# Last block of an S4 + gated FFN kernel: two halves of a slot group transposed apart with zero-padded tables, and a quarter of the residual sum moved to TensorE and ScalarE

## The chip, the cores and the metric

The kernel runs on one core of a Trainium2 chip. The metric is the device time of one execution in microseconds (us); lower is better. Engines are named as in the profile: PE is TensorE (PEld its weight loads), DVE is VectorE, ACT is ScalarE, POOL is GpSimd, SP is SyncE, which here only issues DMAs.

## The reference

`x` is normalised over its 512 channels. Each channel is convolved with its own long kernel `K`, made from 128 complex modes, by FFTs of twice the length; beside it a two-layer GELU network runs on the same normalised input. The output is the input plus the product of the two:

```python
xn = _layernorm(x, axis=-1)
s = _A_ref(xn, ...)    # K[d,l] = Re sum_n C*dt*B * exp(dt*A*l);  y = irfft(rfft(xn) * rfft(K))[:L] + xn * Dskip
g = _silu(_B_ref(xn, w1, b1, w2, b2))    # gelu(xn @ w1 + b1) @ w2 + b2
return x + s * g
```

With L = 2048 rows, D = 512 channels, 128 modes, 1792 hidden units; all in fp32.

## The kernel before, in words

The first part (until about 390 us) runs the network, normalisation and the tables of `K`, in an order written out by hand (`ORDER`). Its result `g` is put in DRAM (`gd`).

The second part does the convolution. Channels are taken in four blocks of 128 (NB = 4), and the FFT is factored as 32 x 64 (N1 x N2). In a block the work goes through eight slots: `second_dft` (L911) makes the spectra of input and kernel on PE, `spectrum` copies one of the two from PSUM to SBUF (ACT, `uh`, L919), `product` and `combine` multiply the spectra on DVE (L929, L937, L939) into `Y`, one `Y` for two slots (`Y_0` to `Y_3`). The way back follows: `back_dft` (L948) transforms `Y_j` on PE into two PSUM banks `sa`; `back_out` (L959) copies them into the SBUF tile `Z` (kh = 0 for j = 0, 1; kh = 1 for j = 2, 3); `turn` (L968) is a DVE transpose of 32 x 32 blocks from `Z` into `T`, in two halves s = 0, 1 (rows q 0 to 7 and 8 to 15 of the output); `last_dft` (L988) multiplies `T` with the table `gc` into the result `y` in PSUM: 16 products, one for each of the 16 parts of 32 x 32 of the PE array (g picks the rows, w the columns), first those of kh = 0, then those of kh = 1 on top. At last `y` is multiplied with `g` (DVE), `x` is added, and the sum is stored.

The order on each engine is that of the code, since the region is recorded with a manual schedule. For blocks 0 to 2 the way back lies beside the next block's slots. For the last block it has nothing beside it, and is written out at the end of the kernel (L1197 to L1243):

- `back_dft` of `Y_3` is cut into two halves (`h0`, `h1`), which write parts of the same two banks, so the second half waits until ACT has copied the first one out.
- The four rows of `y` are cut into two halves of q. The first half has its PSUM tiles `wide` (two for all four channel groups), the second half four banks (`py[1]`).
- `last_dft` of kh = 0 for the first half, four products of the identity with itself that write into a bank that is overwritten next (L1211), `last_dft` of kh = 0 for the second half, and kh = 1 for both.
- On DVE: the copy of one bank of `Y_3`'s second half (L959), the two transposes of kh = 1 (L968), then the products with `g` (`gated`, L1226 and L1223) and half of the additions of `x` (`added`, L1230). The other half of the additions is on POOL (L1230). In `parts(s, n)`, s is the half of q and n the half of the 128 channels; `added(s, 0)` is POOL's, `added(s, 1)` DVE's.
- Stores t = 0, 1 hold the first half of q, t = 2, 3 the second half; t = 0 and 2 are issued by SP, 1 and 3 by ACT.

Of the kernel before, what the change touches and what calls it, by code (L numbers as in the profile page):

```python
# [11 lines left out]
F32 = mybir.dt.float32  # L12
# [8 lines left out]
P = 128  # L21
L, D, NS, F = 2048, 512, 128, 1792
G = D // P
NF = F // P
KD = D // P
N1, N2 = 32, 64
NB = 4
# [5 lines left out]
NQ = L // P  # L33
# [95 lines left out]
def _shape_constants():  # L129
    n1 = np.arange(N1)[:, None]  # L130
    k1 = np.arange(N1)[None, :]
    a = 2 * np.pi * n1 * (k1 + 0.25) / N1
    cf = np.zeros((G, N1, 2, 2, N1))
    for g in range(G):
        cf[g, :, g % 2] = np.stack([np.cos(a), -np.sin(a)], 1)
    cg = np.stack([np.cos(a).T, -np.sin(a).T], 1).reshape(2, 2, 4, 2, 2, N1)
    cg = np.tile(cg.transpose(1, 3, 2, 4, 0, 5).reshape(1, N1, 2, N1), (G, 1, 1, 1))
    n2 = np.arange(N2)[:, None]
    k2 = np.arange(N2)[None, :]
    cm = np.zeros((2, N2, N1, 2, N2))  # L140
    ct = np.zeros((2, N2, N1, 2, N2))
    for k in range(N1):
        th = 2 * np.pi * (n2 * (k + 0.25) / L + n2 * k2 / N2)
        c, s = np.cos(th), np.sin(th)
        cm[:, :, k, 0, :] = c
        cm[:, :, k, 1, :] = s
        ct[0, :, k, 0, :] = c.T / L
        ct[1, :, k, 0, :] = -s.T / L
        ct[0, :, k, 1, :] = s.T / L
        ct[1, :, k, 1, :] = c.T / L  # L150
# [7 lines left out]
    return {  # L158
        "cf": cf.reshape(P, 4 * N1).astype(f),
        "cg": cg.reshape(P, 2 * N1).astype(f),  # L160
        "cm": cm.reshape(P, N1 * 2 * N2).astype(f),
        "ct": ct.reshape(P, N1 * P).astype(f),
        "cb": cb.reshape(CH * NPC, CH * NPH).astype(ml_dtypes.bfloat16),
    }
# [3 lines left out]
def kernel(  # L168
# [5 lines left out]
    V, A, GP, PE, SY = nc.vector, nc.scalar, nc.gpsimd, nc.tensor, nc.sync  # L174
# [613 lines left out]
    def open_mid():  # L788
        SB["pm"] = pm = opened(p2, "pm", "right")
        SB["ps"] = opened(pz, "psm", "left", bufs=2, space=PSUM)  # L790
        SB["tcn"] = pm.tile([P, N1, P], F32, name="tcn")
        SB["tb"] = SB["tcn"].rearrange("p (k o) m -> p k o m", o=2)
        xf[1] = pm.tile([P, 2, 2, N1, N2], F32, tag="X1", name="X1")
        SB["uh"] = pm.tile([P, 2, 2, P], F32, tag="uh", name="uh_0_0", bufs=2)
        SB["t0"] = pm.tile([P, 2, 2, 4, N2], F32, tag="t0", name="t0_0_0", bufs=2)
        SB["gc"] = pm.tile([P, 2, N1], F32, name="gc")
        gx[0] = new_tail(0)
        yy[0, "T", 1] = new_turn(0, 1)

# [141 lines left out]
    def back_dft(b, j, es=slice(0, 4)):  # L941
        if (b, j, "p") not in yy:
            yy[b, j, "p"] = [bank(f"sa{b}_{j}_{a}") for a in range(2)]
        for e in range(4)[es]:
            for o in range(2):
                for a, p in enumerate(yy[b, j, "p"]):
                    r = slice(64 * a, 64 * a + 64)
                    PE.matmul(p[:, e, :], yy[b, j][r, o, e, :], SB["tb"][r, 4 * j + e, o, :],  # L948
                              start=(o == 0), stop=(o == 1), skip_group_check=True)

    def back_out(b, j, es=slice(0, 4), engs=(A, A)):
        kh = j // 2
        if (b, "Z", kh) not in yy:
            yy[b, "Z", kh] = SB["pm"].tile([P, N2, N1 // 2, 2], F32, tag=f"Z{kh}", name=f"Z{b}_{kh}")
        for a, (p, eng) in enumerate(zip(yy[b, j, "p"], engs)):
            k = 8 * (j % 2) + 4 * a
            src = p.rearrange("p k (x c) -> p x k c", c=2)[:, :, es]
            dst = yy[b, "Z", kh][:, :, k:k + 4, :][:, :, es]
            eng.copy(dst, src) if eng is A else eng.tensor_copy(dst, src)  # L959

    def new_turn(b, kh):
        return SB["pm"].tile([P, 4, 2, 8, N1], F32, tag=f"T{kh}", name=f"T{b}_{kh}")

    def turn(b, kh, s):
        if (b, "T", kh) not in yy:
            yy[b, "T", kh] = new_turn(b, kh)
        Z = yy[b, "Z", kh].rearrange("p (w s q) k c -> p w s q (k c)", w=4, s=2)
        V.transpose(yy[b, "T", kh][:, :, s], Z[:, :, s])  # L968

    gx = {}  # L970

# [10 lines left out]
    def last_dft(b, kh, py, q=slice(0, NQ)):  # L982
        T = yy[b, "T", kh].rearrange("p w s q i -> p w (s q) i")
        for w in range(4):
            for g in range(G):
                r, m = slice(g * N1, (g + 1) * N1), slice(w * N1, (w + 1) * N1)
                o = py[g].rearrange("p (q i) -> p q i", i=N1)
                PE.matmul(o[m], SB["gc"][r, kh], T[r, w, q], start=(kh == 0), stop=(kh == 1), skip_group_check=True)  # L988
# [173 lines left out]
    with tc.manual_schedule():  # L1162
        SB["spare"] = False
        open_front()
        z_load(NTB - 1)
        for j in range(4):
            mc_load(j)
        side_skip(0)
        side_turn(1, eng=GP)
        SB["spare"] = True  # L1170
        for p in "S0 F00 S1 S2 F01 S3 L0 F10 L1 A0 F11 A1 L2 L3 A2 A3".split():
            if p[0] == "F":
                k = int(p[1]), int(p[2])
# [12 lines left out]
        z_store(NTB - 1)  # L1186
        SB["spare"] = False
        fa.close()
        open_mid()
        ct_load(0)  # L1190
        SY.dma_start(SB["gc"].rearrange("p h n -> p (h n)"), cg)
        for b in range(NB - 1):
            for i in range(4):
                two_slots(b, i)
        for g in range(8):
            slot(NB - 1, g)
        b = NB - 1  # L1197
        h0, h1 = slice(0, 2), slice(2, 4)
        back_dft(b, 3, h0)
        back_out(b, 3, h0)  # L1200
        wide = [SB["ps"].tile([P, 2, 4 * P], F32, tag="ri", name=f"y{b}_{n}", bufs=2) for n in range(2)]
        py = [[wide[g // 2][:, g % 2, :2 * P] for g in range(G)]]
        halves = [slice(0, NQ // 2), slice(NQ // 2, NQ)]
        back_dft(b, 3, h1)
        back_out(b, 3, h1, (A, V))
        last_dft(b, 0, py[0], halves[0])
        py.append([bank(f"y{b}_{g}_1").rearrange("p e m -> p (e m)")[:, :2 * P] for g in range(G)])
        for s in range(2):
            turn(b, 1, s)
        for n in range(4):  # L1210
            PE.matmul(py[1][0][:, :P], ident, ident, start=True, stop=True, skip_group_check=True)  # L1211
        last_dft(b, 0, py[1], halves[1])
        for s in range(2):
            last_dft(b, 1, py[s], halves[s])
        gt, xt_ = gx[b]
        def parts(s, n):
            return tuple(t[:, halves[s], 64 * n:64 * n + 64] for t in (gt, xt_))

        def gated(s, n):
            if s:  # L1220
                for g in (2 * n, 2 * n + 1):
                    gg = gt[:, halves[1], g * N1:g * N1 + N1]
                    V.tensor_mul(gg, py[1][g].rearrange("p (q i) -> p q i", i=N1), gg)  # L1223
            else:
                gp = parts(0, n)[0].rearrange("p q (g i) -> p g q i", i=N1)
                V.tensor_mul(gp, wide[n][:, :, :2 * P].rearrange("p g (q i) -> p g q i", i=N1), gp)  # L1226

        def added(s, n):
            gv, xv = parts(s, n)
            (V if n else GP).tensor_add(xv, gv, xv)  # L1230

        gated(0, 0)
        added(0, 0)
        gated(0, 1)
        gated(1, 0)
        added(0, 1)
        for t in range(2):
            store(b, t, (SY, A)[t % 2])
        gated(1, 1)
        for n in range(2):  # L1240
            added(1, n)
        for t in range(2, 4):
            store(b, t, (SY, A)[t % 2])  # L1243
    pz.close()
# [32 lines left out]
```

## Time and profile before

| what | value |
|---|---|
| time, median of 3 runs (lowest, highest) | 533.06 us (532.49, 534.91) |
| the profiled execution's own time | 532.96 us |
| its span, first to last instruction | 531.1 us |
| mean granted PE clock | 0.995 |
| share of the span busy: PE, PEld, DVE, ACT, POOL | 97%, 80%, 81%, 74%, 49% |
| last PE product of the kernel starts | 523.0 us |
| second pair of stores issued | 527.1 us |

Times within the profile are counted from the start of the span. A row of the timeline gives the start, the length, the engine with its line, the operation, `out<-in` by the program's names, the shapes, and `x` with the number of instructions merged in it; in brackets stands the idle time of the engine ahead of it and what ended that. Instructions on one engine are pipelined, so two that are merged take less than the sum of their single lengths. Each fp32 product of PE appears as two records (and two weight loads).

### The profile page before, as it was taken

The numbers are of one execution on the slowest core, as the hardware profiler recorded it, in microseconds if no ns is written. First come the engines' busy times: TensorE is split into PE (matmuls) and PEld (weight loads), VectorE is DVE, ScalarE is ACT, GpSimd is POOL, SyncE is SP. The second block draws the span as 40 slices with busy tenths as digits, with TensorE's granted clock in tenths as the row PEclk, the third lists the DMA queues.
The fourth block names the chain that finished last, engine by engine and source line by source line (L and its number), as shares of the span: only waits on it lengthen the run. The fifth ranks groups of instructions, "written<-read, shape, count | busy, mean of one in ns | idle before, by whom it ended". The sixth has DMA issues, their size and how long they took to land.

```text
span 531.1 us, 16527 instructions
## 1 busy us (share of the span) xinstructions
PE 516.4 (97%) x6999; PEld 422.4 (80%) x6999; DVE 429.7 (81%) x726; ACT 390.8 (74%) x556; POOL 260.7 (49%) x384
## 2 busy tenths in 40 slices
PE   8899999999999999999999999999999999999993
PEld 8677787877777777877777787778889998998882
DVE  6989899999998789787875886898257779677896
ACT  3588996999987988888778799799454573663330
POOL 5619478667597569669817175645301002103042
PEclk9999999999999999999999999999999999999998
DMA  7946527762427966418135532591656639542552
GB/s 221 307 121 195 187 94 233 241 199 77 161 80 198 352 215 180 140 29 252 41 108 175 185 59 107 133 176 45 233 209 224 77 102 214 164 166 81 195 193 97
DMA packets 86086, 85.84 MB, mean 162 GB/s; under 512 B 41878, under 2 KB 60698, under 8 KB 84988
## 3 DMA queue, kind: packets, MB, share of 16 engines
q1 hardware_dynamic: 76944, 66.43, 42.3%
q0 software_dynamic: 8768, 17.83, 10.8%
q8 instruction: 55, 0.90, 0.7%
q10 hardware_dynamic: 300, 0.53, 0.3%
q14 instruction: 19, 0.16, 0.1%
HBM read 51.22 MB, written 33.55 MB: 160 GB/s over the span
## 4 chain that ended last, share of the span: by engine, by line
PE 84%; DVE 6%; ACT 3%; POOL 3%; DMA 2%; issue 2%; POOLq 0%; DVEq 0%; ACTq 0%
PE s L911 11%; PE z L287 9%; PE z L289 8%; PE z L288 8%; PE f L248 8%; PE f L250 8%; PE f L249 8%; PE s L889 6%; PE sa L948 6%; PE kg L655 5%; PE ph L591 3%; PE y L988 2%; DMA w1s<-in_B_w_dram 1%; DVE hl L274 1%; PE xT L359 1%
## 5 line engine op out<-in xcount | busy, mean ns | idle before, releaser
L616 POOL TENSOR_TENSOR mm<-mm,rc 128x32 f32<-128x32 f32 (+4 forms) x150 | 97.1, 647 | 11.8
L287 PE MATMUL z<-w2h,hh 128*128 128x512 f32 x224 | 95.6, 427 | 0.0
L248 PE MATMUL f<-xh,w1h 128*128 128x512 f32 x220 | 91.7, 417 | 0.9 <-ACT w1h L231 0.6
L250 PE MATMUL f<-xh,w1l 128*128 128x512 f32 x220 | 87.1, 396 | 2.2 <-DVE w1l L233 1.5
L289 PE MATMUL z<-w2h,hl 128*128 128x512 f32 x224 | 87.7, 392 | 0.1
L288 PE MATMUL z<-w2l,hh 128*128 128x512 f32 x224 | 87.7, 391 | 0.0
L249 PE MATMUL f<-xl,w1h 128*128 128x512 f32 x220 | 86.8, 394 | 0.0
L605 DVE SCALAR_TENSOR_TENSOR ra<-ra,ph 128x512 f32<-128x512 f32 x64 | 43.8, 684 | 19.4 <-ACT ra L599 18.5
L911 PE MATMUL s<-X,mc 64*64 64x128 f32 x1536 | 58.0, 272 | 0.4 <-DVE t L929 0.4
L929 DVE TENSOR_TENSOR t<-s,uh 128x512 f32<-128x512 f32 x64 | 40.9, 684 | 15.1 <-ACT uh L919 11.6
L250 PEld LDWEIGHTS f<-xh,w1l 128*128 128x128 f32 x220 | 41.3, 188 | 12.4 <-DVE w1l L233 2.4
L639 DVE TENSOR_TENSOR e<-mm,ra 128x1024 f32<-128x1024 f32 x32 | 42.7, 1336 | 10.0 <-ACT ra L627 4.2
L248 PEld LDWEIGHTS f<-xh,w1h 128*128 128x128 f32 x220 | 41.5, 189 | 11.4 <-ACT w1h L231 1.1
L262 ACT ACTIVATE f<-f,b1s 128x512 f32<-128x512 f32 x56 | 37.2, 665 | 18.1 <-PE f L250 16.9
L289 PEld LDWEIGHTS z<-w2h,hl 128*128 128x128 f32 x224 | 42.1, 188 | 10.1 <-DVE hl L274 0.5
L613 POOL COPY mm<-rc 128x32 f32<-128x32 f32 x30 | 15.5, 516 | 69.5 <-DVE e L646 39.6
L287 PEld LDWEIGHTS z<-w2h,hh 128*128 128x128 f32 x224 | 42.4, 189 | 8.9 <-issue 0.3
L911 PEld LDWEIGHTS s<-X,mc 64*64 64x64 f32 x1536 | 44.8, 133 | 5.3 <-issue 1.5
L288 PEld LDWEIGHTS z<-w2l,hh 128*128 128x128 f32 x224 | 42.2, 189 | 8.2
L249 PEld LDWEIGHTS f<-xl,w1h 128*128 128x128 f32 x220 | 41.3, 188 | 9.1
L919 ACT COPY uh<-s 128x512 f32<-128x512 f32 x32 | 18.8, 587 | 40.1 <-PE s L911 22.0
L274 DVE TENSOR_TENSOR hl<-f,hh 128x512 fp32r<-128x512 f32 x56 | 37.8, 682 | 10.6 <-ACT hh L268 10.6
(183 smaller groups left out, 1130.9 us busy)
## 6 DMA issues: line engine op xcount, KB each, us to landing
x<-in_A_u_dram SPq DMA_DIRECT2D x8, 512.0 KB
xs<-x SPq DMA_DIRECT2D x8, 512.0 KB
xt_h<-xh POOLq DMA_DIRECT2D x4, 1024.0 KB, 5.7
xt_l<-xl POOLq DMA_DIRECT2D x4, 1024.0 KB, 8.2
kgd<-ko SPq DMA_DIRECT2D x16, 256.0 KB
za<-zo SPq DMA_DIRECT2D x4, 1024.0 KB
xh<-xt_h POOLq DMA_DIRECT2D x4, 1024.0 KB, 6.7
xl<-xt_l POOLq DMA_DIRECT2D x4, 1024.0 KB, 10.0
```

Source lines behind the costliest of these rows:

```text
L248: PE.matmul(p, wh[:, k, :], xh[:, k, :], start=(k == 0), stop=False)
L249: PE.matmul(p, wh[:, k, :], xl[:, k, :], start=False, stop=False)
L250: PE.matmul(p, wl[:, k, :], xh[:, k, :], start=False, stop=(k == KD - 1))
L274: V.tensor_sub(hl, hf, hh)
L287: PE.matmul(z, hh[:, s], wh, start=(f0 == 0 and not rows), stop=False)
L288: PE.matmul(z, hh[:, s], wl, start=False, stop=False)
L289: PE.matmul(z, hl[:, s], wh, start=False, stop=(f0 == FA - 1))
L605: V.scalar_tensor_tensor(ra[:, 0, c], ra[:, 1, c], MAGIC, p, op0=ALU.subtract, op1=ALU.subtract)
L616: GP.tensor_mul(mv[:, :, 0:3:2, w:2 * w], mv[:, :, 0:3:2, 0:w], rc[:, 2 + 2 * i:4 + 2 * i, :].rearrange("p j c -> p c j").unsqueeze(3).to_ ...
L639: V.tensor_mul(e1, m1.unsqueeze(1).to_broadcast([P, 2, CH, N1]), ra[:, :, :, :N1])
L911: PE.matmul(p[ka * 64:(ka + 1) * 64, r, o, :, jj], w, xf[b][h, c, :, k, :], start=(c == 0), stop=(c == 1), skip_group_check=True)
L929: V.tensor_mul(t, p[:, i, :, 1].unsqueeze(1).to_broadcast([P, 2, 2, P]), uh)
```

## The change

The change touches only the end of the last block and one table.

- `cg`, the table behind `gc`, gets four more slices of 32 x 32 (2 to 5) beside the two that it had: for j = 0, 1 and o = 0, 1 a copy of half of kh = 1's table in one half of the rows and zeros in the other. The load of `gc` grows from 32 KB to 96 KB.
- In the last block `back_out` puts slots 4, 5 (j = 2) and slots 6, 7 (j = 3) of kh = 1 into two separate halves of `Z`. `turn_pairs` transposes one half of `Z` for one half of q: four DVE transposes of 128 x 512 stand for two of 128 x 1024. The ones of slots 4, 5 no longer need `Y_3`.
- `last_pairs` multiplies each transposed piece with the two padded tables, e = 0, 1, one after the other into alternate groups of 32 columns of `y`: for a half of q and one j, 32 products of 128 columns. Slots 4, 5 and 6, 7 are added up in PSUM, so there are 4 x 32 such products where there were 2 x 16 of 256 columns.
- On PE the first half's `last_dft` of kh = 0 goes between the two halves of `back_dft` of `Y_3`, and the four identity products are gone.
- ACT, not DVE, copies the second bank of the second half of `Y_3`.
- The addition of `x` for the second half of q, n = 0, is no longer POOL's: PE multiplies the identity with that quarter of `x`, then with the gated product, into one PSUM tile (128 x 512), and ACT copies the sum to SBUF. The addition for the first half of q, n = 1, goes from DVE to POOL. DVE keeps one addition, the last.

PE, at the end of the last block. `sa_3_0` and `sa_3_1` are the two banks of `back_dft` of `Y_3`; `y_0`, `y_1` are the tiles of the first half of q, `y_0_1` to `y_3_1` those of the second half; `T_0` and `T_1` are the transposed tiles of kh = 0 and 1. Before:

```order
L948 MATMUL sa_3_0_7183<-tcn,Y_3_7115 128x128
L948 MATMUL sa_3_1_7184<-tcn,Y_3_7115 128x128
L988 MATMUL y_0_7195<-T_0_7074,gc 32x256 x2
L988 MATMUL y_1_7196<-T_0_7074,gc 32x256 x2
...
L1211 MATMUL y_0_1_7223<-ident 128x128 x4
L988 MATMUL y_0_1_7223<-T_0_7074,gc 32x256
...
L988 MATMUL y_0_7195<-T_1_7227,gc 32x256 x2
...
L988 MATMUL y_3_1_7226<-T_1_7227,gc 32x256
```

Of the change, from the first half of `Y_3`'s products on:

```order
L954 MATMUL sa_3_1_7184<-tcn,Y_3_7115 128x128
L1014 MATMUL y_0_7195<-T_0_7074,gc 32x256 x2
...
L954 MATMUL sa_3_0_7183<-tcn,Y_3_7115 128x128
...
L994 MATMUL y_0_7195<-T_1_7221,gc 32x4x32 x4
...
L1014 MATMUL y_0_1_7258<-T_0_7074,gc 32x256
...
L994 MATMUL y_0_1_7258<-T_1_7221,gc 32x4x32 x2
...
L1264 MATMUL o_7379<-last,ident 128x512
L1267 MATMUL o_7379<-last,ident 128x512
```

Sixteen products moved ahead of the second half of `Y_3`, the identity products on `y_0_1` went, each row of `T_1` now stands for twice as many products of half the width, and two products of the identity with `last` (the tile that holds `g` and `x`) follow at the end.

DVE, from the second transpose of kh = 0 to its last instruction (`Z_1` is the tile `Z` of kh = 1). Before:

```order
L968 STREAM_TRANSPOSE T_0_7074<-Z_0_7061 128x4x256
L959 COPY Z_1_7175<-sa_3_1_7184 128x64x4
L968 STREAM_TRANSPOSE T_1_7227<-Z_1_7175 128x4x256 x2
L1226 TENSOR_TENSOR last<-y_0_7195,last 128x2x8x32
L1226 TENSOR_TENSOR last<-y_1_7196,last 128x2x8x32
L1223 TENSOR_TENSOR last<-y_0_1_7223,last 128x8x32
L1223 TENSOR_TENSOR last<-y_1_1_7224,last 128x8x32
L1230 TENSOR_TENSOR last<-last 128x8x64
L1223 TENSOR_TENSOR last<-y_2_1_7225,last 128x8x32
L1223 TENSOR_TENSOR last<-y_3_1_7226,last 128x8x32
L1230 TENSOR_TENSOR last<-last 128x8x64
```

Of the change:

```order
L978 STREAM_TRANSPOSE T_0_7074<-Z_0_7061 128x4x256
L985 STREAM_TRANSPOSE T_1_7221<-Z_1_7175 128x512 x4
L1254 TENSOR_TENSOR last<-y_0_7195,last 128x2x8x32
L1254 TENSOR_TENSOR last<-y_1_7196,last 128x2x8x32
L1251 TENSOR_TENSOR last<-y_0_1_7258,last 128x8x32
L1251 TENSOR_TENSOR last<-y_1_1_7259,last 128x8x32
L1251 TENSOR_TENSOR last<-y_2_1_7260,last 128x8x32
L1251 TENSOR_TENSOR last<-y_3_1_7261,last 128x8x32
L1258 TENSOR_TENSOR last<-last 128x8x64
```

The copy is gone, the two transposes became four of half the size, and one of the two additions left.

The diff, without the table's shape lines:

```diff
+    pair = np.zeros((G, 2, 2, 2, N1 // 2, N1))
+    for j in range(2):
+        for o in range(2):
+            pair[:, j, o, o] = cg[:, N1 // 2 * j:N1 // 2 * (j + 1), 1]
...
@@ back_out @@
+            if b == NB - 1 and kh:
+                Z = yy[b, "Z", kh].rearrange("p x k c -> p (x k c)").rearrange("p (j x k c) -> p j x k c", j=2, k=N1 // 4, c=2)
+                dst = Z[:, j % 2, :, 4 * a:4 * a + 4, :][:, :, es]
...
+    def turn_pairs(b, j, s):
+        Z = yy[b, "Z", 1].rearrange("p x k c -> p (x k c)").rearrange("p (j w s q) -> p j w s q", j=2, w=4, s=2)
+        T = yy[b, "T", 1].rearrange("p w s q i -> p (w s q i)").rearrange("p (j s w q) -> p j s w q", j=2, s=2, w=4)
+        V.transpose(T[:, j, s], Z[:, j, :, s])
+
+    def last_pairs(b, j, py, s):
+        T = yy[b, "T", 1].rearrange("p w s q i -> p (w s q i)").rearrange("p (j s w q) -> p j s w q", j=2, s=2, w=4)
+        for w in range(4):
+            for g in range(G):
+                r, m = slice(g * N1, (g + 1) * N1), slice(w * N1, (w + 1) * N1)
+                o = py[g].rearrange("p (q e i) -> p q e i", e=2, i=N1)
+                for e in range(2):
+                    PE.matmul(o[m, :, e], SB["gc"][r, 2 + 2 * j + e], T[r, j, s, w], start=False, stop=(j == 1), skip_group_check=True)
...
         back_dft(b, 3, h0)
         back_out(b, 3, h0)
...
+        last_dft(b, 0, py[0], halves[0])
         back_dft(b, 3, h1)
-        back_out(b, 3, h1, (A, V))
-        last_dft(b, 0, py[0], halves[0])
+        for s in range(2):
+            turn_pairs(b, 0, s)
+        back_out(b, 3, h1)
+        last_pairs(b, 0, py[0], 0)
...
-        for s in range(2):
-            turn(b, 1, s)
-        for n in range(4):
-            PE.matmul(py[1][0][:, :P], ident, ident, start=True, stop=True, skip_group_check=True)
         last_dft(b, 0, py[1], halves[1])
         for s in range(2):
-            last_dft(b, 1, py[s], halves[s])
+            turn_pairs(b, 1, s)
+        last_pairs(b, 1, py[0], 0)
+        for j in range(2):
+            last_pairs(b, j, py[1], 1)
...
         gated(0, 1)
+        full = SB["ps"].tile([P, 2, 4 * P], F32, tag="ri", name=f"o{b}", bufs=2)[:, 0].rearrange("p (q i) -> p q i", i=64)
+        PE.matmul(full, ident, parts(1, 0)[1], start=True, stop=False)
         gated(1, 0)
-        added(0, 1)
+        gv, xv = parts(1, 0)
+        PE.matmul(full, ident, gv, start=False, stop=True)
+        A.copy(xv, full)
+        GP.tensor_add(parts(0, 1)[1], parts(0, 1)[0], parts(0, 1)[1])
         for t in range(2):
             store(b, t, (SY, A)[t % 2])
         gated(1, 1)
-        for n in range(2):
-            added(1, n)
+        added(1, 1)
```

More of the change, by code (lines that the diff above doesn't have):

```diff
@@ L137, in _shape_constants @@
     cg = np.tile(cg.transpose(1, 3, 2, 4, 0, 5).reshape(1, N1, 2, N1), (G, 1, 1, 1))
+    pair = np.zeros((G, 2, 2, 2, N1 // 2, N1))
+    for j in range(2):
+        for o in range(2):
+            pair[:, j, o, o] = cg[:, N1 // 2 * j:N1 // 2 * (j + 1), 1]
+    pair = pair.reshape(G, 4, N1, N1).transpose(0, 2, 1, 3)
+    cg = np.concatenate([cg, pair], 2)
     n2 = np.arange(N2)[:, None]
@@ L159, in _shape_constants @@
         "cf": cf.reshape(P, 4 * N1).astype(f),
-        "cg": cg.reshape(P, 2 * N1).astype(f),
+        "cg": cg.reshape(P, 6 * N1).astype(f),
         "cm": cm.reshape(P, N1 * 2 * N2).astype(f),
@@ L795, in open_mid @@
         SB["t0"] = pm.tile([P, 2, 2, 4, N2], F32, tag="t0", name="t0_0_0", bufs=2)
-        SB["gc"] = pm.tile([P, 2, N1], F32, name="gc")
+        SB["gc"] = pm.tile([P, 6, N1], F32, name="gc")
         gx[0] = new_tail(0)
@@ L957, in back_out @@
             src = p.rearrange("p k (x c) -> p x k c", c=2)[:, :, es]
-            dst = yy[b, "Z", kh][:, :, k:k + 4, :][:, :, es]
+            if b == NB - 1 and kh:
+                Z = yy[b, "Z", kh].rearrange("p x k c -> p (x k c)").rearrange("p (j x k c) -> p j x k c", j=2, k=N1 // 4, c=2)
+                dst = Z[:, j % 2, :, 4 * a:4 * a + 4, :][:, :, es]
+            else:
+                dst = yy[b, "Z", kh][:, :, k:k + 4, :][:, :, es]
             eng.copy(dst, src) if eng is A else eng.tensor_copy(dst, src)
@@ L968, in turn @@
         V.transpose(yy[b, "T", kh][:, :, s], Z[:, :, s])
+    def turn_pairs(b, j, s):
+        if (b, "T", 1) not in yy:
+            yy[b, "T", 1] = new_turn(b, 1)
+        Z = yy[b, "Z", 1].rearrange("p x k c -> p (x k c)").rearrange("p (j w s q) -> p j w s q", j=2, w=4, s=2)
[9 more added lines that the diff above has]
+                    PE.matmul(o[m, :, e], SB["gc"][r, 2 + 2 * j + e], T[r, j, s, w], start=False, stop=(j == 1), skip_group_check=True)
     gx = {}
@@ L1198 @@
         h0, h1 = slice(0, 2), slice(2, 4)
+        halves = [slice(0, NQ // 2), slice(NQ // 2, NQ)]
         back_dft(b, 3, h0)
@@ L1202 @@
         py = [[wide[g // 2][:, g % 2, :2 * P] for g in range(G)]]
-        halves = [slice(0, NQ // 2), slice(NQ // 2, NQ)]
+        last_dft(b, 0, py[0], halves[0])
         back_dft(b, 3, h1)
-        back_out(b, 3, h1, (A, V))
-        last_dft(b, 0, py[0], halves[0])
+        for s in range(2):
+            turn_pairs(b, 0, s)
+        back_out(b, 3, h1)
+        last_pairs(b, 0, py[0], 0)
         py.append([bank(f"y{b}_{g}_1").rearrange("p e m -> p (e m)")[:, :2 * P] for g in range(G)])
-        for s in range(2):
-            turn(b, 1, s)
-        for n in range(4):
-            PE.matmul(py[1][0][:, :P], ident, ident, start=True, stop=True, skip_group_check=True)
         last_dft(b, 0, py[1], halves[1])
         for s in range(2):
-            last_dft(b, 1, py[s], halves[s])
+            turn_pairs(b, 1, s)
+        last_pairs(b, 1, py[0], 0)
+        for j in range(2):
+            last_pairs(b, j, py[1], 1)
         gt, xt_ = gx[b]
```

## The prediction

> **What bounds the kernel now.** The change touches only the end of the last block, so I first read the chain of waits from there on. It names, in order of time, the work that each next piece waited for.
>
> ```profile
> 518.17 1.43 PE sa L948 x16
> 519.60 0.64 PE y L988 x32
> 520.24 1.09 PE y L1211 x8
> 521.33 1.41 PE y L988 x59
> ...
> 526.04 0.97 DVE last L1230
> ```
>
> Up to 522.7 the chain stands on PE, then it goes over to DVE, whose last addition ends at 527.0. The lines "PE y" hide who is late: the identity products (L1211) only fill a wait. DVE's timeline shows what PE waits for.
>
> ```profile
> 515.74 1.28 DVE L929 TENSOR_TENSOR t<-s,uh 128x512 f32<-128x512 f32 x2
> ...
> 517.73 1.24 DVE L968 STREAM_TRANSPOSE T<-Z 128x1024 f32<-128x1024 f32 x1
> 519.69 0.42 DVE L959 COPY Z<-sa 128x256 f32<-128x256 f32 x1 [0.72 <-issue]
> 520.22 2.37 DVE L968 STREAM_TRANSPOSE T<-Z 128x1024 f32<-128x1024 f32 x2
> 522.76 1.29 DVE L1226 TENSOR_TENSOR last<-y,last 128x512 f32<-128x512 f32 x2 [0.17 <-PE y L988]
> 523.97 0.74 DVE L1223 TENSOR_TENSOR last<-y,last 128x256 f32<-128x256 f32 x2
> 524.63 0.72 DVE L1230 TENSOR_TENSOR last<-last 128x512 f32<-128x512 f32 x1
> 525.27 0.74 DVE L1223 TENSOR_TENSOR last<-y,last 128x256 f32<-128x256 f32 x2
> 526.04 0.97 DVE L1230 TENSOR_TENSOR last<-last 128x512 f32<-128x512 f32 x1
> ```
>
> From 519.7 DVE never rests: the copy, two transposes (one ready at 521.4, one at 522.6), six products, two additions. So DVE is what ends last, through the transposes first and then by itself. PE, POOL and the stores stand beside it:
>
> ```profile
> 518.17 1.43 PE L948 MATMUL sa<-tcn,Y 64*128 64x128 f32 x16 [0.54 <-ACT Z L959]
> 519.53 0.71 PE L988 MATMUL y<-T,gc 32*32 32x256 f32 x32
> 520.17 1.16 PE L1211 MATMUL y<-ident 128*128 128x128 f32 x8
> 521.26 2.15 PE L988 MATMUL y<-T,gc 32*32 32x256 f32 x96
> 523.53 2.94 POOL L1230 TENSOR_TENSOR last<-last 128x512 f32<-128x512 f32 x2 [11.45 <-DVE last L1226]
> 525.41 2.00 SPq L999 DMA_DIRECT2D out_dram<-last  x2
> 527.08 0.33 SPq L999 DMA_DIRECT2D out_dram<-last  x1
> ```
>
> The first pair of stores is issued at 525.41, the second at 527.08. What a store costs after its issue is in a table by stretches (columns: length, busy time and count of PE, PEld, DVE, ACT, POOL, then granted clock, DMA share, GB/s):
>
> ```profile
> 514.50:517.70 3.20, 3.13 (x60) 2.76 (x49) 3.13 (x7) 1.52 (x3) 0.00 (x0) 1.00 0.97 368
> 526.00:527.60 1.60, 0.00 (x0) 0.00 (x0) 0.98 (x2) 0.00 (x0) 0.47 (x1) 0.54 0.85 320
> 527.80:529.40 1.60, 0.00 (x0) 0.00 (x0) 0.00 (x0) 0.00 (x0) 0.00 (x0) 0.50 0.88 328
> 529.40:531.10 1.70, 0.00 (x0) 0.00 (x0) 0.00 (x0) 0.00 (x0) 0.00 (x0) 0.50 0.00 0
> ```
>
> The bytes of a pair (four stores of 256 KB are two pairs) start 0.7 us after the issue, run for 1.6 us, and the last byte is 1.7 us ahead of the span's end. So the span ends 4.0 us after the second issue: 527.08 + 4.0 = 531.1. If the two pairs came close together, both would run as one stream: at the 368 GB/s of the first row 1.05 MB take 2.85 us, at 328 GB/s 3.2. Then the end is 0.7 + 2.85 + 1.7 = 5.25 (to 5.6) us after the first issue.
>
> **The change part by part.**
>
> *The larger table.*
>
> ```profile
> 396.19 0.33 SPq L1191 DMA_DIRECT2D gc<-in_cg_dram  x1
> 444.49 1.09 PE L988 MATMUL y<-T,gc 32*32 32x512 f32 x25
> ```
>
> 64 KB more on SP's queue, issued 48 us before PE first reads the table. At the 368 GB/s above they are 0.2 us for the loads behind them. Zero.
>
> *The first half's products ahead of the second half of `Y_3`.* PE idles 0.54 us at 517.63 for ACT's copies. The sixteen products cost 0.71, and the next group stood 0.64 after their start (519.53 to 520.17). What they read was done when DVE's products of slot 7 ended at 517.02. They fill 517.55 to 518.2, so `Y_3`'s second half starts where it did or up to 0.1 later, and PE is free at 519.55 rather than 520.2. ACT's copy of the second bank replaces DVE's; by ACT's copy of the first bank (0.37 against 0.42) it ends when that did, 520.1.
>
> ```profile
> 519.43 0.37 ACT L959 COPY Z<-sa 128x256 f32<-128x256 f32 x1 [1.04 <-PE sa L948]
> ```
>
> *The transposes.* The trace has none of 128 x 512. Between a half and a whole of the large one (1.19 each in a row of two), I take 0.6, since other DVE work here halves with its size:
>
> ```profile
> L639 DVE TENSOR_TENSOR e<-mm,ra 128x1024 f32<-128x1024 f32 x32 | 42.7, 1336 | 10.0 <-ACT ra L627 4.2 <-issue 3.9 <-PE kg L655 1.1
> L929 DVE TENSOR_TENSOR t<-s,uh 128x512 f32<-128x512 f32 x64 | 40.9, 684 | 15.1 <-ACT uh L919 11.6 <-issue 3.2
> ```
>
> Two of them (slots 4, 5) fall into DVE's rest of 0.72 and the place of the copy: 518.9 to 520.1. Slots 6, 7 are ready at 520.85 and 521.45, where they were at 521.4 and 522.6. At 1.19 each they would be ready at 522.5 and 523.6, a loss of 1.1.
>
> *The products with the padded tables.* This is the dear part. 32 products become 128 of half the width, so twice the columns; and two in a row go to the same 32 x 32 part of the array, which no row of before does. What the rows show of such parts:
>
> ```profile
> 519.53 0.50 PE L988 MATMUL y<-T,gc 32*32 32x256 f32 x16
> 519.77 0.47 PE L988 MATMUL y<-T,gc 32*32 32x256 f32 x16
> ...
> 503.07 0.23 PEld L988 LDWEIGHTS y<-T,gc 32*32 32x32 f32 x32 [0.17 <-issue]
> 503.52 0.10 PEld L988 LDWEIGHTS y<-T,gc 32*32 32x32 f32 x1 [0.22 <-issue]
> 503.95 0.55 PEld L988 LDWEIGHTS y<-T,gc 32*32 32x32 f32 x31 [0.32 <-issue]
> ```
>
> Each product has two records. The sixteen first records all start from 519.53 on, the sixteen second ones from 519.77 on: a part is held for 0.24 by 256 columns, and a record that must wait for its part is passed by fifteen products for other parts. For 128 columns I take 0.11 (the eight identity records of 128 columns in 1.16 us, less the last one's tail). But after sixteen products (32 loads) the queue takes one load more and stops until the first product is finished (503.95). So I let PE hold sixteen products at a time; a part then does four records in a row, 0.45, and 32 products take two fillings, about 1.05 us in a stream and 1.45 with their tail. Bounds inside this picture: 0.7 if loads go on at the burst's pace, 1.5 if nothing overlaps between groups.
>
> Then: slots 4, 5 first half 519.6 to 520.65; kh = 0 second half (0.5) to 521.2; slots 6, 7 first half, whose transpose is long ready at 520.85, give their result at 522.5 (now 522.7); the two groups of the second half are finished at 524.5, where the last product now ends at about 523.4. So the first half gains 0.25, the second loses 1.1.
>
> *DVE after that.* First products at 522.5 and 523.1; then it waits for PE until 524.5 instead of doing an addition (0.72). Two products to 525.25 (0.74), two more to 525.9, one addition of 0.72 to 0.97: done at 526.9.
>
> *A quarter of the sum on PE and ACT.* The first identity product starts behind PE's groups at 524.6. 512 columns are the 512 of the four identity products (1.16 with tail, 0.9 without): to 525.5. The second must wait for DVE's 525.25 and for PE: 525.5 to 526.65. ACT's copy of 128 x 512 out of PSUM takes 0.59 (L919, below), so the second pair of stores is issued at 527.35, now 527.08.
>
> ```profile
> L919 ACT COPY uh<-s 128x512 f32<-128x512 f32 x32 | 18.8, 587 | 40.1 <-PE s L911 22.0 <-issue 11.4 <-DVE t L929 1.9
> ```
>
> Behind that copy on ACT stand only the stores t = 1 and 3.
>
> *POOL has both additions of the first half.* They start behind the first product: 523.25, and at 2.94 for two end at about 526.1. Today DVE's share is ready at 525.35, so the first pair of stores goes out 0.7 later, at 526.1.
>
> ```profile
> 523.53 1.27 POOL L1230 TENSOR_TENSOR last<-last 128x512 f32<-128x512 f32 x1 [11.45 <-DVE last L1226]
> ```
>
> By the spacing above the end is 526.1 + 5.25 = 531.35; by the second pair it is 527.35 + 4.0 = 531.35. Both ways it is 531.4, **0.3 us later** than now: what DVE gave up is paid back by PE's doubled products, POOL and the crowding of the stores. The profiled execution took 532.96, so the forecast is 533.3; the median shown is 533.06, which that run stands 0.1 below.
>
> Bounds of the same course: with 0.7 for a group the first product is at 521.65, the second half no longer waits for PE, and POOL's two additions, both as short as its first one today, send the stores off at 525.0: end 530.3, time 532.2. With 1.5 for a group: 523.1, second half 526.1, second identity product to 528.2, stores at 528.85, end 532.85, time 534.7.
>
> **The rivals.**
>
> *A. PE at burst pace.* The low bound: 532.2, with POOL as the new end. For it speaks the burst of 32 loads in 0.23 us; against it the stop after them.
>
> *B. Two products in a row on one part stop the ones behind them (slower).* `last_pairs` has e innermost. If PE's queue holds the next part back until the second product's first load is in, each of the 16 pairs of a group costs 0.11 to 0.12, a group 1.95: first half at 524.1, second at 528.0, stores at 530.75, end 534.8, time 536.6. It decides as soon as a group takes over 1.8 us. Against it: records pass a waiting one at 519.53. For it: there, products for other parts pass a product's own second record; that they pass a whole second product no row shows.
>
> *C. The same, but the second product must itself start first.* Then a pair costs two records, 0.24, and a group 3.84: first half at 527.85, second at 535.5, end 542.3, time 544.2. The rows at 519.53 and 519.77 speak against it, as second records start after fifteen later first ones; only if these are not separate entries of the queue can it hold.
>
> The Trainium skill has such a rule: its page "TensorE: Matmul & The Clock Gate", section "Part 3: Packing small matmuls: row/col tiling", says that products start and end strictly in the program's order and that only weight loads are pulled ahead. By that rule the time would be C's. The trace does not agree for fp32 products in two records, as the rows at 519.53 and 519.77 show; whether whole products keep the order, no run here shows.
>
> *D. The change does nothing to the end,* as the second pair of stores is held by something else: nothing in the trace after 527.08 is touched, so I give it no case of its own.
>
> **How the numbers follow.** Under half a per cent, 2.7 us (530.3 to 535.6 on the profiled run), a measurement of this kernel can't be told from no change. Chances: the forecast's own course 0.62 (532.4 to 534.9), A 0.14, B 0.08, C or worse 0.15, 0.01 for something faster that I don't see. The likeliest is 533.3. The range goes from 531.8 to 537.0 and holds the first three, 0.84. Faster by over half a per cent 0.01; within it 0.76; slower 0.23.
>
> **What would show each step.** In the changed profile: the products of 128 columns as four groups of 64 records, each about 1 us long (B: 2, C: near 4); ACT's last copies of `Z` ending at 520.1; four transposes of about 0.7 with the last ready near 521.5; DVE's first product at 522.5 and a wait on PE ahead of the third; POOL's additions ending at 526.1; the first stores later than 525.41 and the gap between the two pairs shrunk from 1.7 us to about 1.2. The forecast is wrong if a group of `last_pairs` takes much over 1.5 us, or if POOL's second addition, beside DVE, takes much longer than 1.7.

## The result, and the profile after

The changed kernel takes 536.71 us (median of 11 runs, 534.92 to 539.0), the kernel before on the same chip 534.08 (11 runs, 532.49 to 534.91). The ratio is 1.0056, with a 95% interval of 1.0039 to 1.0073: slower by 2.1 to 3.9 us, where the forecast was 0.3 us later, not to be told from no change.

The profiled execution took 539.0 us, the longest of the eleven, with a span of 537.2 against 531.1. Most of these 6.1 us lie where nothing was changed. A common mark is the start of the DVE transpose of slots 0 to 3 for the second half of q (in rows of the timeline the last `T<-Z` of 128x1024 ahead of the change, L968 before, L978 after): 517.73 before, 521.53 after. So 3.80 us had gone by then, and **2.30 us** came behind the mark (13.37 before, 15.67 after). All times "from the mark" below are counted so, the ends with spans as shown, to 0.1 us; the 3.80 us are looked at last.

PE of the changed kernel behind the mark, from the timeline:

```profile
523.41 1.15 PE L994 MATMUL y<-T,gc 32*32 32x128 f32 x47
524.30 0.40 PE L1014 MATMUL y<-T,gc 32*32 32x256 f32 x1
524.31 0.27 PE L994 MATMUL y<-T,gc 32*32 32x128 f32 x1
...
525.16 2.37 PE L994 MATMUL y<-T,gc 32*32 32x128 f32 x104
528.43 1.99 PE L994 MATMUL y<-T,gc 32*32 32x128 f32 x84 [0.90 <-issue]
530.35 1.12 PE L1264 MATMUL o<-last,ident 128*128 128x512 f32 x2
531.32 1.02 PE L1267 MATMUL o<-last,ident 128*128 128x512 f32 x2
```

Its weight loads show the same stop more sharply:

```profile
524.95 2.31 PEld L994 LDWEIGHTS y<-T,gc 32*32 32x32 f32 x107
528.43 1.72 PEld L994 LDWEIGHTS y<-T,gc 32*32 32x32 f32 x84 [1.17 <-issue]
```

Two things are new. PE stops for 1.17 us in the middle of a group of `last_pairs`, ahead of its last 84 records, and the profile names no releaser ("issue": the engine waited for nothing that the profile shows). And the pace between stops is 84 records in 1.72 us, 20.5 ns a record.

DVE, POOL, ACT and SP of the same kernel:

```profile
522.69 2.52 DVE L985 STREAM_TRANSPOSE T<-Z 128x512 f32<-128x512 f32 x4
526.73 1.29 DVE L1254 TENSOR_TENSOR last<-y,last 128x512 f32<-128x512 f32 x2 [1.51 <-PE y L994]
530.03 1.45 DVE L1251 TENSOR_TENSOR last<-y,last 128x256 f32<-128x256 f32 x4 [2.02 <-PE y L994]
531.51 0.69 DVE L1258 TENSOR_TENSOR last<-last 128x512 f32<-128x512 f32 x1
```
```profile
527.50 1.26 POOL L1258 TENSOR_TENSOR last<-last 128x512 f32<-128x512 f32 x1 [13.18 <-DVE last L1254]
528.72 1.26 POOL L1269 TENSOR_TENSOR last<-last 128x512 f32<-128x512 f32 x1
```
```profile
532.38 0.58 ACT L1268 COPY last<-o 128x512 f32<-128x512 f32 x1 [8.50 <-PE o L1267]
532.43 0.93 ACTq L1025 DMA_DIRECT2D out_dram<-last  x2
```
```profile
530.01 3.30 SPq L1025 DMA_DIRECT2D out_dram<-last  x2
```

DVE's third product starts at 530.03, 8.51 from the mark; before it was 6.24. From there to the end it takes as long as before (7.16, before 7.13), so the 2.27 us by which DVE's third product is later are the result. ACT's first store (at 532.43) stands behind its copy and goes out 2.4 us after SP's first one.

### The profile page after: what moved, and what is told of

Read it like the earlier page. It is cut to its first block, busy times and chain, and to the rows that moved or that the text cites. A ratio compares the mean times of both kernels' runs of the same rounds, so it can differ in the third digit from the quotient of the medians.

```text
span 537.2 us, 16902 instructions
## 1 busy us (share of the span) xinstructions
PE 522.2 (97%) x7187; PEld 425.8 (79%) x7187; DVE 427.7 (80%) x726; ACT 391.5 (73%) x558; POOL 257.9 (48%) x384
## 4 chain that ended last, share of the span: by engine, by line
PE 84%; DVE 7%; ACT 3%; DMA 2%; issue 2%; POOL 1%; SPq 0%; ACTq 0%; POOLq 0%; DVEq 0%
PE s L917 11%; PE z L293 9%; PE z L295 8%; PE f L256 8%; PE z L294 8%; PE f L254 8%; PE f L255 8%; PE s L895 6%; PE sa L954 6%; PE kg L661 5%; PE ph L597 2%; PE y L1014 2%; PE y L994 1%; DMA w1s<-in_B_w_dram 1%; DMA b2st<-in_B_b_dram 1%
## 5 line engine op out<-in xcount | busy, mean ns | idle before, releaser
L917 PE MATMUL s<-X,mc 64*64 64x128 f32 x1536 | 59.4, 272 | 1.7 <-issue 1.2
L917 PEld LDWEIGHTS s<-X,mc 64*64 64x64 f32 x1536 | 46.3, 133 | 7.3 <-issue 4.4
L619 POOL COPY mm<-rc 128x32 f32<-128x32 f32 x30 | 14.4, 479 | 71.4 <-DVE e L652 41.4
```

What stands on the lines that cost most here:

```text
L917: PE.matmul(p[ka * 64:(ka + 1) * 64, r, o, :, jj], w, xf[b][h, c, :, k, :], start=(c == 0), stop=(c == 1), skip_group_check=True)
```

## The experiments

The theory that the trace suggested, F: PE's program comes in blocks of 256 instructions, the next block is fetched once the one ahead of it has been entered, and the doubled products use up a block before the next is there. Its ground is a count. In the trace one record of a product is two instructions of PE (load and product), and a wait that stands in the queue by itself (EVENT_SEMAPHORE) is one. Counted so, the stops of over 0.45 us in the last 100 us of the changed kernel's span, at which the next instruction waits for no semaphore, stand after 10178, 10433, 12993, 13250 and 14273 instructions: all five are 193 or 194 over a multiple of 256. What matters is the distance between them; why it is 193 and not 0 is not shown, and the count may not begin where the program does. In what follows, such a place is called a border. The DMA view, cut to the time from the entry into the block at 14017 (524.76) to the end of the stop, shows what the 16 DMA engines did then:

```profile
DMA packets 2, 0.02 MB, mean 7 GB/s; under 512 B 0, under 2 KB 0, under 8 KB 0
## 3 DMA queue, kind: packets, MB, share of 16 engines
q8 instruction: 1, 0.02, 2.0%
q14 instruction: 1, 0.01, 0.8%
```

One packet of 16 KB of instructions (16,384 bytes, 64 for each of 256 instructions) is nearly all there was. The other one, 8 KB on q14, is not what PE waited for: the trace of the kernel before has it too, at 523.96, and in `shift16` below it starts at 526.95, after the stop. In the trace the packet of 16 KB starts at 525.79, 1.02 after the entry, takes 1.19, and PE goes on 1.45 after its end: 3.67 us in all. The rival theories: S, the second of two products on one part holds up the queue (the prediction's B); P, the stop belongs to its place in the program, a wait that the profile does not show; Q, the new way to add `x` costs the time.

### e outermost

```diff
-        for w in range(4):
-            for g in range(G):
-                ...
-                for e in range(2):
+        for e in range(2):
+            for w in range(4):
+                for g in range(G):
+                    ...
                     PE.matmul(o[m, :, e], ...)
```

> The changed kernel with the loop over e outermost in last_pairs: no two products in a row go to the same 32 x 32 part. Theory F (PE's program arrives in blocks of 256 instructions and the tail uses a block up faster than the next one comes): the same number of instructions, so the stop of 1.2 us in last_pairs stays, at the same count of instructions, and the time is within 0.5 us of the changed kernel's 536.7. Rival S (the second product on the same part holds up the queue): no stop, a group of 64 records in 0.7 to 1.0 us where it takes 1.3, DVE's third product 1.5 us earlier, time 535.0 to 535.3.

Measured: 535.57 (kernel before in that call 533.55), ratio 1.0045 (1.002 to 1.007). The weight loads:

```profile
520.87 0.78 PEld L994 LDWEIGHTS y<-T,gc 32*32 32x32 f32 x63 [0.23 <-DVE T L985]
...
522.10 1.65 PEld L994 LDWEIGHTS y<-T,gc 32*32 32x32 f32 x108
525.59 1.12 PEld L994 LDWEIGHTS y<-T,gc 32*32 32x32 f32 x84 [1.84 <-issue]
```

Both theories are half right, and both missed the time (F 536.2 to 537.2, S 535.0 to 535.3). The order did cost: the last 84 records take 1.12 us, 13.3 ns each where they took 20.5, and DVE's first product comes 0.73 earlier (4.47 from the mark, 5.20 in the changed kernel). But the stop is at the same count, 14273, and has grown to 1.84: PE reaches the border sooner and waits longer, as the block came 3.75 us after the entry. Of the pace that was won only 0.53 arrives at DVE's third product (7.98), and S's price of 0.12 a pair was too high: it is 4 x (20.5 - 13.3) = 29 ns for the four records of a pair.

### The pairs without the new additions, and the new additions without the pairs

In `pairs_only` the lines from `gated(0, 0)` on are those of before; `sum_only` is the kernel before with the changed kernel's lines there.

> The changed kernel with the additions of x as before the change (no identity product, no copy by ACT, DVE and POOL add two quarters each). Theory F: the stop of 1.2 us is there at the same place; DVE's third product comes about 2.2 us later than in the kernel before, counted from the end of the first half of Y_3's products, and everything behind it as well: 536.2 to 536.8. Rival Q (the moved quarter and ACT's hold on a store cost the time): 534 to 534.6, as before.

> The kernel before with only the new way to add x (identity products, ACT's copy, POOL's second addition in the first half), and the slots 4 to 7 turned together as before. Theory F: PE has no more than some 440 instructions after the block border at 13761 and does not stop, so nothing of the 2.3 us is here: the second pair of stores goes out about 0.5 earlier than in the kernel before, the first one 0.7 later, and the time is 0.5 below to 0.3 above the kernel before. Rival Q (POOL's two additions and ACT's copy, which holds back one store, cost the time): 1 us or more above it.

`pairs_only`: 535.53 against 533.55, ratio 1.0043 (1.0026 to 1.006); from the mark the end is at 15.52, 2.15 later than before. `sum_only`: 534.21 against 533.99, ratio 0.9995 (0.9979 to 1.0011); end at 13.79. The stop is in the first, and not in the second, where PE's loads wait for DVE alone at the end (first `pairs_only`, then `sum_only`):

```profile
524.09 1.72 PEld L994 LDWEIGHTS y<-T,gc 32*32 32x32 f32 x84 [1.08 <-issue]
```
```profile
524.04 1.01 PEld L988 LDWEIGHTS y<-T,gc 32*32 32x32 f32 x64
525.43 0.28 PEld L988 LDWEIGHTS y<-T,gc 32*32 32x32 f32 x32 [0.37 <-DVE T L968]
```

So the pairs cost it, and Q falls as the main cause. F had DVE's third product right in `pairs_only` (2.17 later than before, expected 2.2), but not the time: 536.2 to 536.8 was 0.7 too long. In `sum_only` the second pair of stores goes out 0.43 earlier (8.92 from the mark, 9.35 before), and the end is 0.42 later all the same, as the first pair is 0.65 later (8.33, before 7.68) and all four then queue for the DMA engines: the end comes 5.46 after the first pair.

### The border moved

```diff
+        yy[b, 3, "p"] = [bank(f"sa{b}_3_{a}") for a in range(2)]
+        for n in range(16):
+            PE.matmul(yy[b, 3, "p"][0][:N1, n % 4, :N1], ident[:N1, :N1], ident[:N1, :N1], start=True, stop=True, skip_group_check=True)
         back_dft(b, 3, h0)
```

`shift44` has 44 in place of 16. The small products write where `back_dft` writes next, so they change no result; they add instructions, and PE's time for them.

> The changed kernel with 16 small products (64 instructions, about 0.65 us of PE) ahead of Y_3's first half. Theory F: the stop in last_pairs comes 32 records earlier in the program, so that about 116 records of 128 columns are left behind it where there are 84 now, and lasts 1.3 to 1.6 us; time 0 to 0.7 above the changed kernel's. Rival P (the stop belongs to its place in the program, a bank or a wait that the profile does not show): the stop stays ahead of the last 84 records.

> The changed kernel with 44 small products (176 instructions, about 1.8 us of PE) ahead of Y_3's first half. Theory F: two stops in last_pairs where there is one now: about 1.0 us inside the second half of the first two groups (slots 6, 7 of the first half of q), ahead of some 170 records, and about 1.1 us ahead of the last 45 records; DVE's first product about 1 us later after the end of Y_3's first half, the end about 1.1 later after it, the time 1.1 to 2.9 above the changed kernel's. Rival P: one stop ahead of the last 84 records, nothing later than that.

`shift16` takes 536.84, ratio 1.0068 (1.0049 to 1.0086); `shift44` 540.14, ratio 1.0135 (1.0112 to 1.0158), both against 533.55. Their last stops, first of `shift16`, then of `shift44`:

```profile
526.39 2.32 PEld L994 LDWEIGHTS y<-T,gc 32*32 32x32 f32 x115 [0.85 <-issue]
```
```profile
528.34 2.99 PEld L994 LDWEIGHTS y<-T,gc 32*32 32x32 f32 x148
532.44 1.01 PEld L994 LDWEIGHTS y<-T,gc 32*32 32x32 f32 x43 [1.11 <-issue]
```

With 64 instructions more ahead of it, the stop lies 32 records earlier in the program (116 products' records are left, of which the row shows 115 loads; 84 before); with 176 more it lies ahead of the last 44. By the count it is at 14274 and 14530, again 193 or 194 over a multiple of 256. That settles P: the stop goes with the number of instructions, not with a place. F had the time of `shift16` right (0.1 above the changed kernel's, expected 0 to 0.7) and missed three sizes. In `shift16` the stop lasted 0.85, not 1.3 to 1.6, as the fetch took 3.23 us in all. In `shift44` the first of the two stops did not come: PE needed about 3.0 us for that block, in which some products of `back_dft` still lie, and the packet was in 1.4 us after the entry (2.2 in the changed kernel). And its time is 3.4 above the changed kernel's, expected 1.1 to 2.9: the 44 small products, all on one 32 x 32 part, took 3.01 us of PE, not 1.8.

### The padded tables for the first half of q alone

```diff
...
+                for s in range(2):
+                    ps_ = p.rearrange("p k (w s q c) -> p s w q k c", w=4, s=2, c=2)
+                    A.copy(Zs[s][:, :, :, es], ps_[:, s, :, :, es])
...
-        for s in range(2):
-            turn_pairs(b, 0, s)
+        turn_pairs(b, 0, 0)
...
         last_pairs(b, 1, py[0], 0)
-        for j in range(2):
-            last_pairs(b, j, py[1], 1)
+        last_dft(b, 1, py[1], halves[1])
```

`back_out` puts the first half of q into `Z` by j and the second half in the order of the kernel before (`Zs`), with a copy for each; `turn_pairs(b, 1, 1)` turns the whole second half, 128x1024.

> The changed kernel with the padded tables for the first half of q alone; the second half is turned whole and multiplied by 16 products of 256 columns as before the change, and ACT's copies into Z are cut in two. 192 instructions fewer, so PE enters the last block of 256 and ends 241 instructions later. Theory F: no stop in last_pairs; DVE's third product 5.9 to 6.3 us after the start of the transpose of slots 0 to 3 (changed kernel 8.5, kernel before 6.24), time within 0.5 of the kernel before. Rival S (the pace of two products on one part is all that counts): the first half's groups are as slow as in the changed kernel, and the second half gains 1.3 of its 2.3 us: time 0.7 to 1.2 above the kernel before.

Measured: 535.5 against 533.99, ratio 1.0018 (1.0001 to 1.0034); from the mark the end is at 14.07, 1.60 earlier than in the changed kernel. Loads of PE and the products of DVE:

```profile
521.25 0.98 PEld L1002 LDWEIGHTS y<-T,gc 32*32 32x32 f32 x53
522.45 0.41 PEld L1022 LDWEIGHTS y<-T,gc 32*32 32x32 f32 x24
522.79 1.32 PEld L1002 LDWEIGHTS y<-T,gc 32*32 32x32 f32 x55
524.26 0.51 PEld L1022 LDWEIGHTS y<-T,gc 32*32 32x32 f32 x17
```
```profile
524.57 1.29 DVE L1260 TENSOR_TENSOR last<-y,last 128x512 f32<-128x512 f32 x2 [0.94 <-PE y L1002]
525.77 1.41 DVE L1257 TENSOR_TENSOR last<-y,last 128x256 f32<-128x256 f32 x4
```

There is no stop, and DVE no longer waits ahead of its third product (6.54 from the mark). F's range of 5.9 to 6.3 was missed by 0.24, as the first half's groups keep the slow pace (S) and DVE's first product comes at 5.34. The time, above the kernel before by 0.96 by the ratio and 1.5 by the medians, is S's (0.7 to 1.2) rather than F's (within 0.5). So F is right on the stop and S on the pace. What is left of the loss, 0.70, is that and the late first stores (8.63).

### Two versions meant to be better

`quarter_first` is the kernel before, with the identity products and ACT's copy for the first half of q, n = 1; POOL adds both quarters n = 0. `best` is `half0_pairs` with e outermost and these additions; `half0_e_old_sums` has the additions of the kernel before instead.

> The kernel before with one quarter of x, that of the first half of q, n = 1, added by the identity products and copied out by ACT; POOL adds the two quarters n = 0, DVE one. Theory F: no stop; the first pair of stores goes out at about the same time as in the kernel before, the second pair 0.7 to 0.9 earlier, as DVE has an addition less; the end is 0.4 to 0.8 earlier: ratio to the kernel before 0.9985 to 0.9993. Rival Q: 1 us or more above the kernel before.

> half0_pairs with the loop over e outermost and with the additions of quarter_first. Theory F: no stop, a group of last_pairs at 13 ns a record, DVE's first product about 0.4 us earlier than in the kernel before and the third one too; first stores at about 7.1 us after the start of the transpose of slots 0 to 3 (kernel before 7.7), second pair at 8.3 (9.35): end 0.6 to 1.0 earlier than in the kernel before, ratio 0.998 to 0.999. Rival S: no better than quarter_first.

> The kernel with the padded tables for the first half of q alone and the loop over e outermost, with the additions of x as in the kernel before. Theory F, with what the stores have shown (the end comes 5.4 us after the first pair of stores where all four go out together, 4.0 after the second pair where they don't): no stop; DVE's first product 4.65 us after the start of the transpose of slots 0 to 3, so all behind it 0.37 earlier than in the kernel before: first stores at 7.3, second pair at 9.0, end at 13.0 (kernel before 13.37), ratio 0.999 to 1.000. Rival T (what the additions gave or took does not matter, the turned pairs cost by themselves): end at 13.4 or later, as in the run with quarter_first's additions.

`quarter_first`: 534.11 against 533.99, ratio 1.0005 (0.9988 to 1.0022), end at 13.81 from the mark: the gain did not come. The second pair of stores is 0.45 earlier (8.90), the first one 0.73 later (8.41), because the way over PE and ACT is long: DVE's product ends at 524.88, and ACT's copy, which the stores wait for, at 526.95, 2.07 us later. `best`: 534.73 against 533.99, 1.0014 (0.9998 to 1.003), end at 13.46; PE and DVE are as foreseen (first product 4.66, third 5.87), and the same late first stores (8.08) eat it; it is no better than `quarter_first`, as S had said. `half0_e_old_sums`: 533.84 against 533.92, ratio 1.0 (0.9987 to 1.0012); its DVE and SP rows:

```profile
522.60 1.29 DVE L1260 TENSOR_TENSOR last<-y,last 128x512 f32<-128x512 f32 x2 [0.23 <-PE y L1002]
...
525.88 0.97 DVE L1264 TENSOR_TENSOR last<-last 128x512 f32<-128x512 f32 x1
```
```profile
525.24 2.01 SPq L1033 DMA_DIRECT2D out_dram<-last  x2
```

From the mark (517.93): first product 4.66, stores 7.31 and 8.98, end 12.97, 0.40 earlier than before, as expected. The gain shows in the trace alone; it is less than the runs can tell from none. By this one execution rival T falls: the pairs, with half the instructions and in the better order, cost nothing.

### ACT's store ahead of its copy

```diff
-        A.copy(xv, full)
         GP.tensor_add(parts(0, 1)[1], parts(0, 1)[0], parts(0, 1)[1])
         for t in range(2):
             store(b, t, (SY, A)[t % 2])
+        A.copy(xv, full)
```

> The changed kernel with the first pair of stores issued ahead of ACT's copy, so that ACT's store t = 1 no longer stands behind a copy that waits for PE. Theory F (the stop and the pace of PE set the end): both first stores at about 8.5 us after the start of the transpose of slots 0 to 3, the end 0 to 0.2 earlier than in the changed kernel (15.67): 15.45 to 15.7. Rival H (the held store and the crowd of three stores at the end cost a part of the 2.3): the end at 15.1 or earlier.

Measured: 535.28 against 533.92, ratio 1.0034 (1.0019 to 1.0048); end at 15.17 from the mark, nearly H's number and out of F's range. But most of it is not H's mechanism:

```profile
524.87 1.72 PEld L994 LDWEIGHTS y<-T,gc 32*32 32x32 f32 x84 [0.81 <-issue]
```

The stop was 0.81 in this execution where it was 1.17, and DVE's third product so 0.37 earlier (8.14). Behind the last stores the end comes after 4.03, in the changed kernel after 4.24 and in the kernel before after 4.03 (by the spans of the traces to 0.01 us, by which the end is at 15.12, 0.57 earlier). The held store thus costs about 0.2 us; the other 0.37 is the shorter fetch.

## Why the prediction was wrong, step by step

- *DVE's four transposes and ACT's copies.* Right: the last transpose ends 3.68 from the mark (522.69 + 2.52 = 525.21; forecast 521.5, or 3.77).
- *The first half's products ahead of `Y_3`'s second half.* Right. What they read was ready earlier than the prediction says, with the transpose that starts at 512.56 in the kernel before, and not with slot 7's products at 517.02; that changes nothing in the sum.
- *The pace of `last_pairs`, "about 1.05 us in a stream".* Too short. It was worked out from columns and a filling of sixteen products; it is 64 x 20.5 ns = 1.31, and the order of e costs a third of that (13.3 ns with e outermost). Two groups too long by 0.26 each account for DVE's first product being 0.43 late: 5.20 from the mark, forecast 4.77.
- ***The step that failed*** is the next one, "the two groups of the second half are finished at 524.5". It let PE run on as long as its queue and its inputs allowed. The runs showed another limit, to which the prediction gave no time: the program itself. At the six stops in the tail, 3.2 to 3.75 us lie between the entry into one block of 256 instructions and the first instruction of the next. The four groups have 512 instructions, where the two of before had 128, and PE went from the border at 14017 to the next in 2.4 us (524.76 to 527.15), with e outermost in 1.8. DVE's third product came at 8.51, forecast 6.77: 0.43 from the first product on, and 1.31 from the second half, nearly all of it the stop.
- *DVE, PE and ACT after that.* Right: 2.95 from the third product to the second pair of stores, forecast 2.85.
- *POOL with both additions of the first half.* Right: first store at 8.48, forecast 8.37. That ACT's store waits behind the copy was named, but not priced: about 0.2 at the end.
- *The end after the last stores.* 4.21, forecast 4.0.

Sum: 1.74 + 0.10 + 0.21 = 2.05, and 15.67 less the forecast's 13.62 is 2.05. The bound of 1.5 us for a group (534.7 in time) covered the pace, not the stop. The prediction also took a change under half a per cent for one that can't be told from none; with eleven runs each the interval of the ratio is 0.17% to either side.

The rivals: B's time, 536.6, is the measured one, but its mechanism is not. A second product on the same part costs 29 ns a pair rather than 120. That the measured time lies in the range of the prediction, which B's time had stretched upwards, is luck. C is excluded, as a group takes 1.31 us and not 3.84. The Trainium skill has the rule that products start strictly in the program's order ("TensorE: Matmul & The Clock Gate", "Part 3: Packing small matmuls: row/col tiling"); the trace does not agree with the rule: in the rows at 524.30 and 524.31 a product of L1014, which stands behind the whole first group, starts while 17 records of that group are still to come. They belong to at most 15 other parts, so on one of these at least a whole product, with both its records, was still to come.

Still open is why the fetch takes 3.23 us in one run and 3.75 in another; nothing was tried on the fetch itself.

**The 3.80 us ahead of the mark** are for the most part stops at borders too, and which execution loses how much there looks like chance. PE's code is the same there, and so are the borders. From the entry into the block at 9921 (441.5 to 444.6 in the span) to the mark, the twelve profiled executions (ten runs, before and after) take 75.1 to 78.8 us. Without what PE lost at the borders in between (each gap between two loads there, less 0.1) they take 74.6 to 74.9, all twelve: the kernel before lost 0.5 there, the changed kernel 3.9, `shift16` 2.3, `sum_only` 1.3, and `e_outer`, whose code is the changed kernel's up to the tail, 0.9. Two of the stops of the changed kernel:

```profile
448.12 0.30 PEld L917 LDWEIGHTS s<-X,mc 64*64 64x64 f32 x9 [1.00 <-issue]
...
452.89 0.75 PEld L895 LDWEIGHTS s<-fc,in 64*128 64x128 f32 x12 [0.83 <-issue]
```

In the kernel before, the packet for the first of these borders started 1.01 after the entry into the block ahead and took 0.96; in the changed kernel it started 2.34 after it and took 1.51. From 444.9 to 446.7 there, around that packet, the queue of the other DMAs moved 699 packets, 694 of them under 512 bytes. That they made the packet late was not tried.

## What to carry to other kernels

Count the instructions of a dense stretch of small products, not their columns: an fp32 product of 32 x 32 is four instructions, and where PE had to wait in the tail, a block of 256 instructions came 3.2 to 3.75 us after the entry into the one ahead of it, however few columns the products had. If PE stops with no releaser, count from the last such stop: a multiple of 256 (to within one in such a count) points to this cause, and adding some instructions ahead of it tests it, since the stop then comes earlier in the code by as many. In the last microseconds ask first when the first stores go out, since all bytes behind them queue.

## What the runs showed of the hardware

- PE's program arrives in packets of 16 KB. From the border at 9921 on, in all twelve profiles, the packet for the next block starts 0.2 to 3.1 us after PE enters the one before it and takes 0.9 to 1.8; where PE stopped for it, PE uses it 1.3 to 1.9 after its end. The Trainium skill ("Runtime: NRT & Kernel Launch", section "Instruction fetch mechanics") says that the next 16 KiB are fetched while the current ones are executed, and that crossing a border is mostly hidden. The traces agree on the size and on one block ahead; nearly hidden it was at the last borders of the kernel before (0.38 us between two loads at the worst of them), not in the tail of the changed kernel and five of its variants (stops of 0.81 to 1.84 in six profiles), and not at every border ahead of the mark either (1.13 between two loads at the worst of the changed kernel).
- Products of PE for other parts of the array pass whole products that wait, not only their second records (rows at 524.30).
- Two products in a row on one 32 x 32 part slow the stream from 13.3 to 20.5 ns a record (the last 84 records of `e_outer` and of the changed kernel).
- Four stores of 256 KB that go out within 0.6 us end 5.4 us after the first; in two pairs 1.7 us apart they end 4.0 us after the second.
